# Attention followed by a mixture of experts: routing moved into attention, rows scattered to a table sorted by expert, layer one with stationary weights

## The chip, the cores and the metric

One core of one Trainium2 chip. The metric is device time in microseconds (us) of one execution; the kernel before takes 1046.56 us (median of four runs, 1046.24 to 1047.22). Each kernel was also run once under the hardware profiler; all readings of lines, waits and windows are from that execution. Its span is some 2 us shorter than the time of the run. All runs compared here are in the same state (fast).

## The reference, cut to what matters

```python
# attention: B, H, S, D = 8, 8, 576, 64, causal, with a bias from cumulated s
x = attention(q, k, v, s)                 # brought to (8, 576, 512): 4608 tokens of 512 numbers
logits = x @ w_gate                       # (512, 8): eight experts
local  = sigmoid(x @ w_local)             # (512, 1)
for b in range(8):
    prev_e = -1
    for s in range(576):
        fresh = argmax(logits[b, s])
        e = fresh if s == 0 or local[b, s] < 0.5 else prev_e   # a token may keep its neighbour's expert
        prev_e = e
        p = softmax(logits[b, s])
        out[b, s] = p[e] * (relu(x[b, s] @ w1[e]) @ w2[e])      # w1: 512 x 1024, w2: 1024 x 512, fp32
```

Which expert a token has is known only after its batch is through attention, and where it stands among its expert's tokens only after the batches before it were counted. With these inputs they fill 41 blocks of up to 128 tokens of one expert each (the prediction counts them).

## The kernel before, in its parts that matter

Attention runs over 32 pairs of heads and writes x to a table in device memory, in the order of tokens. Then `route` works on all eight batches at once, mostly on VectorE, and makes four tables for 43 blocks (the largest number that there can be): expert of a block, indices to gather by, indices to scatter by, gates. Then the experts' loop:

```python
def gather(i):                                   # rows of block i, one index for each row, by GpSimd
    xg[i] = gp.tile([P, D], F32, name="xg")
    nc.gpsimd.indirect_dma_start(out=xg[i][:, :], out_offset=None, in_=x_d[:, :],
                                 in_offset=bass.IndirectOffsetOnAxis(ap=idx_g[:, i : i + 1], axis=0))

def layer1(i, half):                             # x stationary, 512 columns of w1 move
    # ... (cut)
    for c in range(DK):
        mm(ps, lhsT=xT[i][:, c, :], rhs=ws[i][0][:, c, f], start=(c == 0), stop=(c == DK - 1))
    nc.scalar.activation(hs[i][:, f], ps, Act.Relu)

def turn_h(i):                                   # eight transposes of h, then copies out of PSUM
    # ... (cut)

def layer2(i):
    # ... (cut) 8 matmuls of 512 columns into ps
    nc.vector.tensor_scalar_mul(y, ps, gate[:, i : i + 1])
    nc.gpsimd.indirect_dma_start(out=out[:, :], ..., in_=y[:, :], ...)   # scatter of y, also by GpSimd

for i in range(NBLK):                            # NBLK = 43
    load(i + 2)                                  # w1 and w2 of the block, 2 MB each, issued by SyncE
    gather(i + 3)
    layer1(i + 1, 0)
    turn_h(i)
    turn_x(i + 2)                                # four transposes of the gathered rows
    layer1(i + 1, 1)
    layer2(i)
```

Note the distance between `gather(i + 3)` and the use of its rows: they are turned by `turn_x(i + 3)`, in the next turn of the loop.

## Time and profile before

| part of the span (1044.4 us) | from, to (us) | what it does |
|---|---|---|
| attention | 0 to 321.7 | TensorE full |
| routing | 321.7 to 378.7 | TensorE mostly idle, half clock |
| experts | 378.7 to 1029.7 | 43 blocks of some 15.05 us, TensorE full |
| tail | 1029.7 to 1044.4 | last y, its scatter, its landing |

The lines for this table are in the prediction. One more reading of the kernel before is wanted for what follows: how long a gather has. Its timeline, TensorE and GpSimd lines picked out (start, length, engine, line, operation, out<-in, count, and in brackets the idle time before with what ended it):

```profile
617.95 0.98 POOL L841 DMA_INDIRECT xg<-x_tokens,idx_g  x1 [0.30 <-issue]
...
619.71 0.60 PE L850 MATMUL xp<-ident,xg 128*128 128x128 f32 x4
...
634.76 0.60 PE L850 MATMUL xp<-ident,xg 128*128 128x128 f32 x4
```

The turn at 619.71 is of an older block; the rows asked for at 617.95 are turned at 634.76. That leaves 16.8 us, and a gather lands in 11.0 as a rule. Its table of waits has one wait of TensorE for gathered rows in the whole run, at the first block (3.4 us).

### The profile page before, as it was taken

The page shows a single profiled execution, that of the slowest core. Times are in us where ns is not written, and L with a number is a line of the kernel's source. Part 1 is how long each engine was busy: PE and PEld are TensorE (multiplying, and loading weights), DVE is VectorE, ACT ScalarE, POOL GpSimd, SP SyncE. Part 2 cuts the span into 40 slices and gives each one's busy share as a digit, 9 for nine tenths or more (in the row PEclk, how much of TensorE's full clock was granted, in tenths as well). Part 3 has the DMA queues.
Part 4 walks back from the last instruction along what each step waited for, and adds up shares of the span by engine and source line. Part 5 has one row for each costly group of instructions (what it writes and reads, how often), then busy time and mean ns, then how long its engine had stood idle before and what let it go on. Part 6 is the DMA issues. An engine that isn't in the chain of part 4 may idle for free.

```text
span 1044.4 us, 12912 instructions
## 1 busy us (share of the span) xinstructions
PE 992.7 (95%) x5028; PEld 593.4 (57%) x5028; DVE 204.7 (20%) x562; ACT 228.0 (22%) x549; POOL 160.4 (15%) x278
## 2 busy tenths in 40 slices
PE   8999999999995659999999999999999999999994
PEld 6778778788884624444444444444444444444441
DVE  3222222222225511111111111111111111111110
ACT  4445454554540001110111111011101110111010
POOL 2212212221220310110111011101111110111000
PEclk9999999999997569999999999999999999999997
DMA  9546336337011089877877887788778778877820
GB/s 283 199 116 220 136 100 225 139 92 228 1 46 46 1 336 427 315 302 304 346 299 289 323 334 286 302 334 314 298 303 347 302 296 312 345 288 301 316 95 3
DMA packets 42934, 249.35 MB, mean 239 GB/s; under 512 B 16845, under 2 KB 16877, under 8 KB 29168
## 3 DMA queue, kind: packets, MB, share of 16 engines
q1 hardware_dynamic: 33952, 226.72, 57.9%
q0 software_dynamic: 7008, 20.74, 5.1%
q10 hardware_dynamic: 1904, 0.98, 0.4%
q8 instruction: 42, 0.69, 0.3%
q14 instruction: 28, 0.23, 0.1%
HBM read 229.54 MB, written 20.71 MB: 240 GB/s over the span
## 4 chain that ended last, share of the span: by engine, by line
PE 92%; DMA 2%; DVE 2%; SPq 2%; POOL 0%; issue 0%; ACT 0%; POOLq 0%; DVEq 0%; ACTq 0%
PE hp L862 29%; PE yp L878 28%; PE po L294 14%; PE ps L243 9%; PE htp L871 4%; PE pot L306 2%; PE xp L850 2%; PE table L795 2%; DMA vTb<-in_vT_dram 2%; SPq L143 1%; DMA w1b<-in_w_dram 1%; PE pot L310 1%; PE vwp L210 1%; PE ps L249 1%; PE vwt L222 0%
## 5 line engine op out<-in xcount | busy, mean ns | idle before, releaser
L862 PE MATMUL hp<-w1b,xT 128*128 128x512 f32 x688 | 312.4, 597 | 5.3 <-DMA w1b<-in_w_dram 4.7
L878 PE MATMUL yp<-w2b,hT 128*128 128x512 f32 x688 | 302.4, 593 | 0.3 <-ACT hT L872 0.3
L878 PEld LDWEIGHTS yp<-w2b,hT 128*128 128x128 f32 x688 | 130.9, 190 | 164.4 <-issue 163.8
L862 PEld LDWEIGHTS hp<-w1b,xT 128*128 128x128 f32 x688 | 128.5, 192 | 151.0 <-issue 149.5
L254 ACT ACTIVATE sc<-ps,bias 128x320 f32<-128x320 f32 (+3 forms) x384 | 151.1, 487 | 158.6 <-PE ps L249 105.2
L863 ACT ACTIVATE hs<-hp 128x512 f32<-128x512 f32 x86 | 51.4, 597 | 613.2 <-PE hp L862 613.2
L294 PEld LDWEIGHTS po<-va,sc 128*128 128x128 f32 x1280 | 147.7, 192 | 20.5 <-issue 20.3
L294 PE MATMUL po<-va,sc 128*128 128x74 f32 x1280 | 156.8, 278 | 0.0
L881 POOL DMA_INDIRECT out_dram<-y,idx_s x43 | 43.6, 1013 | 564.8 <-DVE y L880 564.8
L880 DVE TENSOR_SCALAR y<-yp,gate 128x512 f32<-128x512 f32 x43 | 32.3, 751 | 401.6 <-PE yp L878 401.6
L243 PE MATMUL ps<-qb,kb 64*128 64x320 f32 (+3 forms) x768 | 110.2, 407 | 0.0
L260 POOL TENSOR_SCALAR_AFFINE_SELECT sc<-sc 128x256 f32<-128x256 f32 (+1 forms) x96 | 47.3, 493 | 247.5 <-ACT sc L254 247.5
L243 PEld LDWEIGHTS ps<-qb,kb 64*128 64x128 f32 x768 | 61.9, 189 | 17.5 <-issue 1.9
L872 DVE COPY hT<-htp 128x512 f32<-128x512 f32 x43 | 29.8, 692 | 156.1 <-PE htp L871 156.1
L871 PEld LDWEIGHTS htp<-ident,hs 128*128 128x128 f32 x344 | 40.3, 141 | 22.6 <-issue 22.6
L298 DVE RECIPROCAL recs<-po 128x4 f32<-128x4 f32 x64 | 11.7, 183 | 198.2 <-PE po L294 198.2
L871 PE MATMUL htp<-ident,hs 128*128 128x128 f32 x344 | 44.6, 273 | 0.0
L841 POOL DMA_INDIRECT xg<-x_tokens,idx_g x43 | 42.0, 976 | 13.4 <-issue 13.4
L852 DVE COPY xT<-xp 128x512 f32<-128x512 f32 x43 | 29.3, 681 | 15.2 <-PE xp L850 15.2
L795 PE MATMUL table<-val,place 128*128 128x86 f32 x80 | 17.8, 425 | 12.6 <-POOL val L793 12.6
L850 PE MATMUL xp<-ident,xg 128*128 128x128 f32 x172 | 26.3, 276 | 3.4 <-DMA xg<-x_tokens,idx_g 3.4
L300 DVE TENSOR_TENSOR xb<-po,recs 128x256 f32<-128x256 f32 x64 | 27.2, 425 | 2.2
(131 smaller groups left out, 322.0 us busy)
## 6 DMA issues: line engine op xcount, KB each, us to landing
w1b<-in_w_dram SPq DMA_DIRECT2D x43, 2048.0 KB, 13.4
w2b<-in_w_dram SPq DMA_DIRECT2D x43, 2048.0 KB, 8.3
x_tokens<-xb SPq DMA_DIRECT2D x8, 1024.0 KB, 4.9
qb<-in_q_dram SPq DMA_DIRECT2D x7, 1152.0 KB, 5.2
kb<-in_k_dram SPq DMA_DIRECT2D x7, 1152.0 KB, 7.6
vTb<-in_vT_dram SPq DMA_DIRECT2D x7, 1152.0 KB, 9.8
va<-in_vm_dram SPq DMA_DIRECT2D x7, 1024.0 KB, 7.6
qb<-in_q_dram SPq DMA_DIRECT2D x4, 288.0 KB, 4.7
```

The lines of the kernel that those rows point to most:

```text
L243: mm(ps[:, h, at : at + q1 - q0], lhsT=kb[d, hp, c * P : c * P + P], rhs=qb[d, hp, q0:q1], start=True, stop=True)
L254: nc.scalar.activation(sc[:, h, a:z], ps[:, h, a:z], Act.Exp, bias=bias[:, i : i + 1], scale=scale)
L260: nc.gpsimd.affine_select(out=x, in_=x, compare_op=Alu.is_ge, fill=0.0, base=0, pattern=[[0, 2], [0, len(diag)], [1, P]], channel_multipli ...
L294: mm(po[:, t % 2, h, :], lhsT=weights(n, c, t, h), rhs=va[:, c, 2 * hp + h, :], start=(c == 0), stop=(c == t))
L795: mm(table.rearrange("p k b -> p (k b)"), lhsT=place[:, m - c0, :], rhs=val[:, m].rearrange("p k b -> p (k b)"), start=(m == 0), stop=(m = ...
L841: nc.gpsimd.indirect_dma_start(out=xg[i][:, :], out_offset=None, in_=x_d[:, :], in_offset=bass.IndirectOffsetOnAxis(ap=idx_g[:, i : i + 1] ...
L850: tr(ps[:, c, :], x[:, c * P : (c + 1) * P], ident)
L862: mm(ps, lhsT=xT[i][:, c, :], rhs=ws[i][0][:, c, f], start=(c == 0), stop=(c == DK - 1))
L863: nc.scalar.activation(hs[i][:, f], ps, Act.Relu)
L871: tr(ps[:, j, :], h[:, (g + j) * P : (g + j + 1) * P], ident)
L878: mm(ps, lhsT=h[:, c, :], rhs=ws[i][1][:, c, :], start=(c == 0), stop=(c == FK - 1))
L881: nc.gpsimd.indirect_dma_start(out=out[:, :], out_offset=bass.IndirectOffsetOnAxis(ap=idx_s[:, i : i + 1], axis=0), in_=y[:, :], element_o ...
```

## The change: its intent and its core

The intent is to take the 57 us of routing off the path, two blocks off the 43, and the turns of h off each block:

- Routing is cut into stages and runs for batches 0 to 2 and 3 to 5 inside attention, for batches 6 and 7 inside the first expert steps.
- Rows are scattered, with their index and gate in two more columns, to a table sorted by expert. A block then is 128 contiguous rows, fetched by a plain copy.
- The first block of each of four experts ("early") is complete after six batches, so the experts can start while the last two batches are still being routed. 41 blocks always run, the last two only if needed.
- In layer one the weights are stationary and 128 columns of x move. h comes out already transposed.

```diff
-    attention(tc, q, k, vm, vt, vT, s, w_gate, w_local, x_d, ident, lg, recs)
-    route(tc, ident, lg, ebi, idx_g, idx_s, gate)
-    in_range(tc, recs, out_of)
-    experts(tc, w1, w2, out, x_d, ident, ebi, idx_g, idx_s, gate)
+        for bs, n0, each in (((0, 1, 2), 13, 3), ((3, 4, 5), 25, 3)):
+            g = sort.group(bs, xs)
+            for i, (n, half) in enumerate(((n0, 1), (n0 + 1, 0), (n0 + 1, 1), (n0 + 2, 0), (n0 + 2, 1))):
+                at(n, half, g.stages[i])               # five stages, one in each half step of attention
+            for i, f in enumerate(g.scatters):
+                at(n0 + 3 + i // each // 2, i // each % 2, f)   # then `each` scatters in each half step
+    # ... (cut)
+        experts(tc, w1, w2, out, rows_d, ident, sort,
+                [("early", e) for e in range(EARLY)] + [("further", i) for i in range(SURE)], hooks, wf, first)
+    # ... (cut) the last blocks, under conditions
@@ experts
-    def gather(i):
-        nc.gpsimd.indirect_dma_start(out=xg[i][:, :], out_offset=None, in_=x_d[:, :], ...)
+    def fetch(i):
+        # ... (cut) the block's first row, from a table
+            nc.gpsimd.dma_start(xg[i], rows_d[bass.ds(row, P), :])
@@ layer1
-            mm(ps, lhsT=xT[i][:, c, :], rhs=ws[i][0][:, c, f], start=(c == 0), stop=(c == DK - 1))
-        nc.scalar.activation(hs[i][:, f], ps, Act.Relu)
-    def turn_h(i): ...
+        for j in range(4):
+            f = slice((g + j) * P, (g + j + 1) * P)
+            for c in range(DK):
+                mm(ps[:, j, :], lhsT=w[:, c, f], rhs=xT[i][:, c, :], start=(c == 0), stop=(c == DK - 1))
@@ layer2
         for c in range(FK):
-            mm(ps, lhsT=h[:, c, :], rhs=ws[i][1][:, c, :], start=(c == 0), stop=(c == FK - 1))
+            mm(ps, lhsT=h[:, c, :], rhs=w[:, c, :], start=(c == 0), stop=(c == FK - 1))
+            if c == FK // 2 - 1:
+                turn_x(i + 2)
@@ the loop
-    for i in range(NBLK):
+    for i in range(NBL):
         load(i + 2)
-        gather(i + 3)
         layer1(i + 1, 0)
-        turn_h(i)
-        turn_x(i + 2)
+        fetch(i + 2)
         layer1(i + 1, 1)
         layer2(i)
```

## The prediction

> **What bounds the kernel now.** I read the page first (busy shares, slices), then the table of windows, then the groups, the timeline and the chain for durations, last the DMA landings.
>
> ```profile
> PE 992.7 (95%) x5028; PEld 593.4 (57%) x5028; DVE 204.7 (20%) x562; ACT 228.0 (22%) x549; POOL 160.4 (15%) x278
> PE   8999999999995659999999999999999999999994
> PEclk9999999999997569999999999999999999999997
> ...
> 300.00:320.00 20.00, 20.00 (x193) 17.25 (x189) 4.72 (x21) 8.85 (x24) 5.06 (x16) 1.00 0.01 2
> 320.00:330.00 10.00, 4.57 (x42) 2.72 (x40) 6.20 (x25) 0.49 (x2) 0.00 (x0) 0.81 0.36 118
> 330.00:340.00 10.00, 3.12 (x9) 1.72 (x9) 6.51 (x18) 0.61 (x1) 0.00 (x0) 0.50 0.00 0
> 340.00:350.00 10.00, 1.22 (x6) 1.22 (x6) 7.80 (x16) 0.00 (x0) 3.88 (x4) 0.50 0.00 0
> 350.00:360.00 10.00, 10.00 (x48) 9.88 (x47) 3.75 (x5) 0.00 (x0) 3.13 (x5) 0.50 0.01 2
> 370.00:380.00 10.00, 2.43 (x6) 1.56 (x7) 0.69 (x1) 0.00 (x0) 2.84 (x3) 0.50 0.97 374
> ...
> 600.00:700.00 100.00, 100.00 (x297) 49.13 (x296) 14.28 (x21) 11.69 (x21) 13.92 (x14) 1.00 0.81 314
> ```
>
> Columns of a window: length, then busy time and count of PE, PEld, DVE, ACT, POOL, then clock, DMA share, GB/s. TensorE is the bound in attention (to 321.7 us) and in the experts (from 378.7). Between lies routing, 57 us in which TensorE has little to do and runs at half clock; its busy 350 to 360 is the table matmuls at that clock.
>
> ```profile
> 316.36 4.66 PE L294 MATMUL po<-va,sc 128*128 128x74 f32 x40
> 393.31 0.88 PE htp L871 x8
> 394.19 0.44 PE xp L850 x4
> 394.62 3.44 PE hp L862 x8
> 1014.50 6.87 PE yp L878 x16
> 1029.70 0.75 DVE L880 TENSOR_SCALAR y<-yp,gate 128x512 f32<-128x512 f32 x1 [6.67 <-PE yp L878]
> ```
>
> These are start, length, what, count. One block of 128 tokens costs TensorE 16 layer-one passes (2 x 3.44), 8 turns of h (0.88), 4 turns of x (0.44) and 16 layer-two passes (6.87): 15.07 us. Check: from the first layer-one matmul at 378.7 to the last matmul's end, about 1029.7, are 651 us; 43 x 15.04 = 647, plus some 4 for a cold start. After 1029.7 come 14.7 us of tail (y, its scatter, its landing, the reading of the condition).
>
> **What the Trainium skill says.** (1) "TensorE: Matmul & The Clock Gate", section "LDWEIGHTS (loading the stationary operand)": a load takes columns / 1.2 ns, 107 ns for 128. The trace agrees with it as a spacing: the 40 attention matmuls above, each with new 128-column weights and only 74 moving columns, are (4.66 - 0.28) / 39 = 0.112 us apart (0.278 is the mean of one in the groups), and the turns 0.88 / 8 = 0.110. A record's 190 ns is latency. (2) The same page, Part 1, says that an idle window of about 3.4 us brings the clock to half; the trace has 0.50 from 330 us. (3) "DMA: Bandwidth & Descriptors", "Queues, rings and completion order": an engine takes turns between queues packet by packet. The gathers below agree: 4.2 us when nearly alone, 11.0 as a rule, beside the weights' stream. (4) Its section "SWDGE vs HWDGE vs iDMA" has plain copies from GpSimd go through the same software-made descriptors as indirect ones; nothing in this trace separates the two well.
>
> ```profile
> DMA to landing us min/median/max: 4.2/11.0/12.8
> w1b<-in_w_dram SPq DMA_DIRECT2D x43, 2048.0 KB, 13.4
> w2b<-in_w_dram SPq DMA_DIRECT2D x43, 2048.0 KB, 8.3
> out_dram<-y,idx_s POOLq DMA_INDIRECT x43, 8.5
> wbd<-in_w_gate_dram POOLq DMA_DIRECT2D x2, 8.0 KB, 6.9
> ```
>
> The first line is that of the tile xg, the others give issuer, count, size and median us to landing.
>
> **The change, part by part.**
>
> Blocks. Before, 43 are always run. I counted the tokens of each expert with the reference and its inputs: 573, 516, 565, 575, 717, 459, 513, 690. Rounded up to 128 they make 41 blocks. Each of the four early experts has over 128 tokens in the first six batches, so early blocks add none, and 4 + 37 = 41 is just what runs without a condition; both conditional parts are skipped. Two blocks less: -30 us.
>
> Layer one. Weights stationary gives h already transposed: 64 passes of 128 columns in place of 16 of 512 (two passes for each fp32 matmul). A pass of 512 takes 0.429, so 128 columns stream in 0.107; the load of new weights for each pass, at 0.110 to 0.112, is as long and lies beside the pass before. So 64 x 0.111 = 7.1 against 6.87. The 8 turns of h go: -0.88. A block becomes 7.1 + 0.44 + 6.87 = 14.4 us, 0.64 less; over 41 blocks -26 us. If loads did not hide, it would be near 64 x 0.22 = 14; the 0.112 spacing speaks against it.
>
> Routing. Six batches are routed in attention, where DVE is 28% busy and POOL 19%. TensorE itself gets, per group, 10 + 5 small transposes and 4 matmuls, some 2 us. Each of the ten stages can also hold it for about half a microsecond, by banks taken from the scores' three or by DVE's queue; and batches 4 and 7 reuse a row buffer whose scatters were issued within a step, some 2 us each. I put attention at +10, ending at 332. The store of x goes, and nothing waited for it on TensorE.
>
> Transition. In place of 57 us there is the first fetch. Its buffer lies over attention's, so it is issued after the last attention matmul: 0.3 + issue 0.7 + landing about 5.5 (the first gathers took 4.2 and 8.6) + turns at half clock 1.1 + copy 0.9 = 8.5. First layer-one matmul at 340.5. The gain against 378.7 is 38 us.
>
> Last group and first blocks. Two batches are routed between layer-one steps: 15 transposes, some waits, 5 us. Ten scatters, eight fills and the tables have until the fetch of block 4, over 30 us later, so I expect no wait there.
>
> Weights. Now one tile for w1 and w2, freed only by layer two: load i+2 has one period to bring w1, first in the queue. The first in the queue lands in 8.3 us today, so it does not bind. Bytes per block stay the same: the DMA share would go from 0.81 to 0.85.
>
> Tail. One more condition is read by all engines: 14.7 + 4 = 18.7.
>
> Sum without fetch stalls: 340.5 + 41 x 14.4 + 4 + 5 + 18.7 = 958.6; a run is 2.2 longer than its span: 961.
>
> **The rivals.**
>
> (a) The fetch takes over as the bound of each block. Before, row gathers ran three blocks ahead and were never waited for after the first. Now fetch i+2 stands in GpSimd's order behind the scatter of y of block i-1, and is used in the middle of layer two of block i, 7.1 + 3.4 = 10.5 us after the block began. y takes 1 us, the scatter's issue 1.0, the register's load about 0.6, so it is issued at 2.8 and has 7.7 us. A gather's 11.0 would give a wait of 3.3 us in 37 blocks, +122 us, 1083: slower. Rows of 2056 bytes, not 2048, may make it worse. For a shorter landing speak that the fetch is a plain copy of contiguous rows (a plain GpSimd copy landed in 6.9, small and at the start), and that the turn was moved to the middle of layer two, late enough that it looks fitted to a landing that was watched. I can't settle it from this trace. I choose landing near 8 us and charge 0.3 us to each of 37 blocks, +11.
>
> (b) Weight loads do not hide beside 128-column passes fully: at 0.125 per pass a block is 0.9 longer, +37 us, 1009.
>
> (c) Attention stalls more than I give it: Pool's masks behind scatters, a buffer of rows late. At 2 us in each of 20 half steps, +40, 1010. For it: scatters stand in Pool's queue before the masks. Against: values run one step after scores, so masks have several us of slack.
>
> **Range and chances.** 961 + 11 = 972. The low end is no stall and a cheap transition, 945. The high end has a fetch stall near 2 us, 961 + 74 = 1035. Over 2% faster is under 1025.6: only (a) at nearly full size or two rivals together miss it. Faster 0.86, within 2% 0.08, slower 0.06.
>
> **What would show it.** Right: TensorE at 9 in every slice after one short dip near 335 us; layer-one passes at 0.11 spacing and 14.4 to 14.7 us per block; 64 x 41 layer-one records; no htp. Wrong in (a): turns of x with idle before them released by the DMA of xg, some 37 times, and a block of 16 to 18 us; (b): blocks long without idle time on TensorE; (c): attention ending after 340. A low clock beyond the transition, or the conditional blocks being run, would also break the sum.

## The result, and the profile after

| | median of fast runs, us | range | ratio to before |
|---|---|---|---|
| before | 1046.56 | 1046.24 to 1047.22 | |
| after | 1111.56 | 1109.98 to 1121.75 | 1.064 (1.0586 to 1.0695) |

A ratio here is the mean time of one kernel's fast runs over that of the other's of the same rounds, with a 95% interval, so not quite the ratio of the medians. The change made the kernel 6.4% slower; the prediction was 972 us, with a range to 1035.

The page of the profile after (busy us, share of the span, count; then busy tenths in 40 slices of 28 us; then shares of the chain that ended last; a group with busy us, mean ns | idle before, releaser; two landings with KB each and median us):

```profile
span 1120.1 us, 16042 instructions
...
PE 968.3 (86%) x6538; PEld 710.3 (63%) x6538; DVE 210.6 (19%) x649; ACT 181.8 (16%) x465; POOL 173.9 (16%) x333
...
PE   8999998999989978888888787878888897879785
...
PEclk9999999999998989999999999899999888999898
...
DMA out_dram<-y,at 28%; PE yp L1039 2%; DMA xg<-x_rows 1%; POOLq L1001 1%; PE hp L1027 1%; POOL out_dram L1045 0%; POOL x_rows L937 0%; DVE y L1044 0%; POOLq L1045 0%; PE xp L1010 0%; POOLq L118 0%; POOLq L1003 0%
...
L1010 PE MATMUL xp<-ident,xg 128*128 128x128 f32 x164 | 30.0, 313 | 126.2 <-DMA xg<-x_rows 126.2
...
w<-in_w_dram SPq DMA_DIRECT2D x82, 2048.0 KB, 13.5
xg<-x_rows POOLq DMA_DIRECT2D x41, 257.0 KB, 11.4
```

The hole of routing is gone from the slices (the digits 5, 6 and 5 before, none so low after but the tail's), but from slice 14 on, where the experts are, TensorE has mostly 7 and 8 where it had 9. No engine took its place: DVE, ACT and POOL stand under 20%. The DMA engines did not either; one window in the experts (columns as in the prediction) has their share at 0.66, where before it was 0.81 in a like stretch:

```profile
500.00:600.00 100.00, 83.85 (x485) 60.67 (x484) 11.72 (x21) 3.58 (x6) 9.48 (x12) 0.97 0.66 253
```

The chain on the page leads astray: it puts 28% on the scatters of y, follows them one behind the other, and has only 1% for the fetch. It followed GpSimd's own order back from the end. The table of waits, by tile, says it plainly (us in total, times, longest):

```profile
PE xp L1010 <- DMA xg<-x_rows: 126.2, 38, 6.5
```

TensorE waits 38 times for fetched rows, 126.2 us in all: once for the very first rows (3.8 us, before layer one begins) and 37 times within the blocks (122.4 us). The timeline of a block and a half shows why:

```profile
637.12 3.60 PE L1039 MATMUL yp<-w,hT 128*128 128x512 f32 x8
...
644.97 0.88 PE L1010 MATMUL xp<-ident,xg 128*128 128x128 f32 x4 [4.25 <-DMA xg<-x_rows]
...
645.65 5.08 PE L1039 MATMUL yp<-w,hT 128*128 128x512 f32 x8
...
650.56 7.31 PE L1027 MATMUL hp<-xT,w 128*128 128x128 f32 x64
...
650.76 0.75 DVE L1044 TENSOR_SCALAR y<-yp,xg 128x512 f32<-128x512 f32 x1 [4.12 <-PE yp L1039]
651.79 0.99 POOL L1045 DMA_INDIRECT out_dram<-y,at  x1 [19.00 <-DVE y L1044]
652.78 0.59 POOL L1003 DMA_DIRECT2D xg<-x_rows  x1
```

A block begins at 650.56 with layer one. Only then is the y of the block before ready (650.76), GpSimd issues its scatter (651.79), and the fetch stands behind that scatter in GpSimd's program (652.78). It landed 10.8 us later, at 663.6. TensorE wanted the rows after 7.3 us of layer one and half of layer two, at about 661. This is a closed loop: the end of a block starts the fetch that the middle of the next waits for, so the wait returns in every block and can't be worked off.

The line at 645.65 shows a second cost: after the wait of 4.25 us, eight passes of layer two take 5.08 us; the eight ahead of it, at 637.12, took 3.60. Half clock followed the wait: the trace's record of the granted clock has 0.50 from 645.2 to 648.6.

**Where the time went**, by stages of the two profiled runs:

| stage | before | after | difference |
|---|---|---|---|
| to the first layer-one matmul | 378.7 | 338.9 | -39.8 |
| from there to the last layer-two matmul's end | 651.0 | 768.6 | +117.6 |
| tail | 14.7 | 12.6 | -2.1 |
| span | 1044.4 | 1120.1 | +75.7 |

The 768.6 are 41 blocks of 14.45 us (592.5; the period of a block without a wait, from the first experiment), 122.4 of waits for rows, 2.3 for weights, 3 of cold start, 38.7 of half clock after waits, and some 10 that I did not take apart, the last group's routing among them. The half clock is read from the trace's record of the granted clock: after the cold start TensorE worked 77.4 us of this stage at 0.50, and half of that is lost. Of the 36 blocks that follow the wait for block 4, 19 have such a stretch of half clock and take 19.15 to 21.16 us; the other 17 take 16.66 to 18.45.

### The profile page after: what moved, and what is told of

Read it like the earlier page. It is cut to its first block, busy times and chain, and to the rows that moved or that the text cites. A ratio compares the mean times of both kernels' runs of the same rounds, so it can differ in the third digit from the quotient of the medians.

```text
span 1120.1 us, 16042 instructions
## 1 busy us (share of the span) xinstructions
PE 968.3 (86%) x6538; PEld 710.3 (63%) x6538; DVE 210.6 (19%) x649; ACT 181.8 (16%) x465; POOL 173.9 (16%) x333
## 4 chain that ended last, share of the span: by engine, by line
issue 33%; DMA 29%; PE 2%; POOLq 1%; POOL 0%; DVE 0%
DMA out_dram<-y,at 28%; PE yp L1039 2%; DMA xg<-x_rows 1%; POOLq L1001 1%; PE hp L1027 1%; POOL out_dram L1045 0%; POOL x_rows L937 0%; DVE y L1044 0%; POOLq L1045 0%; PE xp L1010 0%; POOLq L118 0%; POOLq L1003 0%
## 5 line engine op out<-in xcount | busy, mean ns | idle before, releaser
L1039 PE MATMUL yp<-w,hT 128*128 128x512 f32 x656 | 329.5, 651 | 0.0
L1027 PEld LDWEIGHTS hp<-xT,w 128*128 128x128 f32 x2624 | 302.1, 193 | 22.7 <-issue 21.3
L1027 PE MATMUL hp<-xT,w 128*128 128x128 f32 x2624 | 303.6, 277 | 3.2 <-DMA w<-in_w_dram 2.3
L1039 PEld LDWEIGHTS yp<-w,hT 128*128 128x128 f32 x656 | 131.9, 211 | 141.6 <-issue 141.6
L1045 POOL DMA_INDIRECT out_dram<-y,at x41 | 40.8, 996 | 673.0 <-DVE y L1044 620.5
L1010 PE MATMUL xp<-ident,xg 128*128 128x128 f32 x164 | 30.0, 313 | 126.2 <-DMA xg<-x_rows 126.2
L307 PE MATMUL ps<-qk 64*128 64x320 f32 (+3 forms) x768 | 110.3, 406 | 0.3 <-ACT sct L329 0.3
L1030 DVE TENSOR_SCALAR hT<-hp 128x512 f32<-128x512 f32 x41 | 28.4, 692 | 251.7 <-PE hp L1027 251.7
L307 PEld LDWEIGHTS ps<-qk 64*128 64x128 f32 x768 | 61.1, 187 | 18.1 <-issue 1.7
L1044 DVE TENSOR_SCALAR y<-yp,xg 128x512 f32<-128x512 f32 x41 | 30.8, 751 | 149.5 <-PE yp L1039 149.5
L937 POOL DMA_INDIRECT x_rows<-xb,r_slot_i x32 | 31.5, 984 | 9.1 <-issue 8.0
## 6 DMA issues: line engine op xcount, KB each, us to landing
xg<-x_rows POOLq DMA_DIRECT2D x41, 257.0 KB, 11.4
```

The lines of the kernel that those rows point to most:

```text
L307: mm(ps[:, h, at : at + q1 - q0], lhsT=kb[d, hp, c * P : c * P + P], rhs=qb[d, hp, q0:q1], start=True, stop=True)
L937: self.s.nc.gpsimd.indirect_dma_start(out=next(self.s.views)[:, :], out_offset=bass.IndirectOffsetOnAxis(ap=self.slot[:z, m : m + 1], axis=0),
L1010: tr(ps[:, c, :], xg[i][:, c * P : (c + 1) * P], ident)
L1027: mm(ps[:, j, :], lhsT=w[:, c, f], rhs=xT[i][:, c, :], start=(c == 0), stop=(c == DK - 1))
L1030: nc.vector.tensor_scalar_max(hT[i][:, g : g + 4], ps, 0.0)
L1039: mm(ps, lhsT=h[:, c, :], rhs=w[:, c, :], start=(c == 0), stop=(c == FK - 1))
```

## The experiments

My theory: the fetch is issued too late for how long it takes beside the weights' stream, and all else in the change is worth what the sum said. The rival: stationary weights, or the routing within attention, cost more than was thought. The first four went to one chip together, the other three to another together (the kernel before: 1047.28 and 1046.64 us there).

### e2_order: the scatter of y issued behind the next fetch

GpSimd's program was: scatter y0, scatter y1, fetch 4, scatter y2, fetch 5, and so on. With the scatter of y moved one turn back, it is: scatter y0, fetch 4, scatter y1, fetch 5. Each fetch is issued one block earlier, and nothing else changes.

```diff
 def layer2(i):
-        y = gp.tile([P, D], F32, name="y")
+        y = ys[i] = gp.tile([P, D], F32, name="y")
         nc.vector.tensor_scalar_mul(y, ps, xg[i][:, D + 1 : D + 2])
-        nc.gpsimd.indirect_dma_start(out=out[:, :], ..., in_=y[:, :], ...)
+    ys = {}
+    def put(i):
+        y = ys.pop(i)
+        nc.gpsimd.indirect_dma_start(out=out[:, :], ..., in_=y[:, :], ...)
 for i in range(NBL):
     load(i + 2)
     layer1(i + 1, 0)
     fetch(i + 2)
+    if i:
+        put(i - 1)
     layer1(i + 1, 1)
     layer2(i)
+put(NBL - 1)
```

> The changed kernel with one order turned round: the scatter of y of block i-1 is issued by GpSimd after the fetch of block i+2, not before it. No buffer, no byte and no TensorE instruction is added. Theory (the fetch is issued too late for its landing of 11.4 us): the fetch no longer waits for y, it goes out nearly a block earlier, the waits of the turns of x for the DMA of xg (130 us in 39 times) go but for block 4, whose rows must first be scattered, and with them the half clock that follows them; a block falls from 18.5 to 14.5 us and the run from 1111 to 955 to 975 us. Rival (the sixteen DMA engines can't carry weights, rows and y of a block in 14.5 us, the late fetch only shows it): blocks stay above 17 us, waits move to the weights w, the time stays above 1080.

Measured: 962.15 us (955.94 to 966.62), ratio 0.9176 (0.913 to 0.9223), right result. Its waits, its window and its timeline:

```profile
PE xp L1010 <- DMA xg<-x_rows: 3.7, 1, 3.7
```

```profile
500.00:600.00 100.00, 100.00 (x580) 72.88 (x579) 15.36 (x28) 4.18 (x7) 11.06 (x14) 1.00 0.84 324
```

```profile
652.95 7.31 PE L1027 MATMUL hp<-xT,w 128*128 128x128 f32 x64
...
655.17 0.59 POOL L1003 DMA_DIRECT2D xg<-x_rows  x1
...
663.53 0.60 PE L1010 MATMUL xp<-ident,xg 128*128 128x128 f32 x4
...
663.97 3.60 PE L1039 MATMUL yp<-w,hT 128*128 128x512 f32 x8
```

The 38 waits have become one, that for the first rows (a wait for block 4, which I had expected, did not come); in this window TensorE is full at full clock, and the DMA share is 0.84, as before the change. The rows asked for at 655.17 are now for the turn one block later, at 678: 22.8 us instead of some 8. Thirty-six blocks in a row take 14.45 us each. Turning the order of two instructions on GpSimd took the loss away.

### e3_turn_late: the other end of the same distance

The issue stays late, and the rows are turned after seven of layer two's eight chunks instead of four, 2.6 us later.

```diff
-            if c == FK // 2 - 1:
+            if c == FK - 2:
                 turn_x(i + 2)
```

> The changed kernel with the turn of x of block i+2 moved from after 4 of the 8 chunks of layer two to after 7 of them: needed 2.6 us later, nothing else moved, no DMA touched. Theory (the wait is landing minus need: 3.1 us now): waits fall to 0.5 us or less, too short to bring the clock down, the copy of xT then costs some 0.3 us of its own before layer one; blocks of 15.0 to 15.5 us, the run at 980 to 1010 us. Rival (DMA throughput): no change, above 1090. Rival (the landing itself follows the period): waits stay near 3 us.

Measured: 989.5 us (986.66 to 997.95), ratio 0.9457 (0.9403 to 0.9511), right result.

```profile
PE xp L1010 <- DMA xg<-x_rows: 18.6, 23, 3.8
```

Of 126.2 us of waits 18.6 are left: 3.8 for the first rows, the others between 0.2 and 1.5 us, so about half of them above the 0.5 that was expected. So giving 2.6 us more at the end of the distance takes nearly all of it away, without touching the order on GpSimd. The waits were a shortage of some 3 us in each block, no more.

### e4_half_weights: the landing without the full weights' stream

Only w1 of each block is loaded; layer two uses the first block's w2. The result is wrong (relative error 1.32).

```diff
-    for a, src in ((0, w1), (DK * F, w2)):
+    for a, src in ((0, w1), (DK * F, w2))[: 1 if half else 2]:
@@ load
-        ws[i] = (wf if wf and i % 3 == 0 else wp).tile(...)
-        load_weights(nc, ws[i], w1, w2, j)
+        ws[i] = wp.tile(...)
+        load_weights(nc, ws[i], w1, w2, j, half=wf is not None)
@@ layer2
-        w = ws[i][:, DK * F :]
+        w = (first if wf else ws[i])[:, DK * F :]
```

> Wrong result on purpose: in the first 41 blocks only w1 is loaded for each block, layer two uses the w2 of the first expert throughout. The order of issues is that of the changed kernel. Theory (the fetch lands late because its packets take turns with the packets of the weights' stream, sent at the same moment): with half the stream the fetch lands some 3 to 5 us earlier, near 7 us from issue, the waits fall under 0.5 us and the run to 955 to 985 us. Rival (a GpSimd copy behind the scatter of y needs 11 us of its own): landing stays at 11, run near 1110.

Measured: 967.67 us (963.58 and 971.76), ratio 0.9237 (0.919 to 0.9284). Waits and window:

```profile
PE xp L1010 <- DMA xg<-x_rows: 8.4, 2, 4.6
```

```profile
500.00:600.00 100.00, 100.00 (x584) 73.26 (x583) 14.98 (x28) 4.18 (x7) 11.09 (x14) 1.00 0.51 178
```

With the weights' traffic halved the fetch, issued as late as in the changed kernel, is in time; the two waits left are for the first rows (3.8 us) and for block 4 (4.6 us). From the trace's records of single packets, a fetch is 64 packets of 4112 bytes (two rows of 2056). In the changed kernel, in e2_order and in e3_turn_late alike, its first packet comes 6.5 us after the issue and its last at about 10.4 (medians); here the first comes at 1.6 and the last at 2.8, earlier than the 7 us that I had expected.

The same records show what the fetch stands behind. The 64 packets of the scatter of y, issued 1 us before it, run first in the same queue: in the changed kernel from 3.5 to 6.6 us after the fetch's issue, here from 0.6 to 1.2. In the kernel before, a gather stood behind a scatter in the same way (128 packets, from 3.2 to 10.0 us). While the fetch's own packets run, about 1.3 packets of weights, 16 KB each, go for one of them. That fits turns taken packet by packet; what the first 3.5 us are spent on stays open. e2_order left this as it is: its fetch still stands behind a scatter, only one block earlier.

What this doesn't settle: since layer two no longer holds the tile, it is free half a block sooner, and the load's place in time moves too. Here a fetch runs with no weights in flight at all. So the weights' stream makes the landing long; what the scatter's packets ahead of the fetch cost by themselves, no run has tested.

### e5_before_layer1: stationary weights alone, on the kernel before

```diff
-            mm(ps, lhsT=xT[i][:, c, :], rhs=ws[i][0][:, c, f], start=(c == 0), stop=(c == DK - 1))
-        nc.scalar.activation(hs[i][:, f], ps, Act.Relu)
+        for j in range(4):
+            f = slice((g + j) * P, (g + j + 1) * P)
+            for c in range(DK):
+                mm(ps[:, j, :], lhsT=ws[i][0][:, c, f], rhs=xT[i][:, c, :], start=(c == 0), stop=(c == DK - 1))
+        # relu into hT, one half on ScalarE and one on VectorE
-            turn_h(i)
```

> The kernel before with layer one alone changed: weights stationary, 64 passes of 128 columns in place of 16 of 512, and the turns of h gone; 43 blocks, gathers and routing as before. Theory (each pass 0.112 us, loads hidden): a block from 15.05 to 14.45 us, 43 x 0.6 = 26 us less, 1046.6 to about 1021. Rival (loads of weights don't hide or the denser stream lowers the clock): same or slower.

Measured: 1021.0 us (1019.96 to 1024.04), ratio 0.9742 (0.9726 to 0.9759), right result: 26 us less, as the prediction's own term for this part has it.

```profile
500.00:600.00 100.00, 100.00 (x580) 73.22 (x579) 14.25 (x20) 3.75 (x7) 13.93 (x14) 1.00 0.83 324
```

580 matmul records in 100 us where the kernel before has about 297, and TensorE full at full clock: loads of new weights for each pass do hide. This is against the prediction's rival (b), and against stationary weights as the cause of the loss.

### e6_before_41: two blocks less, on the kernel before

```diff
-NBLK = N // P + E - 1
+NBLK = N // P + E - 1 - 2
```

> The kernel before with 41 blocks in place of 43, nothing else (valid for these inputs, whose tokens fill exactly 41 blocks). Theory: two blocks of 15.05 us less, 1046.6 to 1016.5; the tables of the routing get 4 columns narrower, under 1 us. Rival (empty blocks are cheap, or the last blocks hide something): less than 20 us gained.

Measured: 1015.71 us (1014.69 to 1016.46), ratio 0.9703 (0.9688 to 0.9718), right result (these inputs need 41 blocks; in general this is no correct kernel). 31 us less.

With the first experiment the parts add up: -31 for two blocks, -25 for layer one (0.60 for each of 41 blocks), and the first layer-one matmul of e2_order at 344.4 instead of 378.7, -34. That is -90 against -85 measured. The difference lies mostly in the first blocks of e2_order, one of which takes 21.12 us: from 376 to 381 us single matmuls of layer one stand over 1 us apart there, released by nothing that the profile shows, and half clock follows.

### e7_spread: e2_order, and the scatters spread over more half steps

In e2_order attention ends later than before, by 16.7 us, about 10 of it in the half steps in which three scatters each are issued. (The profiles of the five runs with this same attention have 11.2 to 19.1.) The changed kernel's timeline shows one such place:

```profile
188.42 0.98 POOL L937 DMA_INDIRECT x_rows<-xb,r_slot_i  x1 [0.28 <-issue]
...
189.71 0.97 POOL L937 DMA_INDIRECT x_rows<-xb,r_slot_i  x1 [0.30 <-issue]
190.98 0.97 POOL L937 DMA_INDIRECT x_rows<-xb,r_slot_i  x1 [0.30 <-issue]
191.97 0.43 POOL L324 TENSOR_SCALAR_AFFINE_SELECT sc<-sc 128x256 f32<-128x256 f32 x1
192.46 1.77 PE L359 MATMUL po<-va,sc 128*128 128x74 f32 x7 [3.71 <-POOL sc L324]
```

Three scatters stand one behind the other on GpSimd at 1.3 us each, the mask of the scores comes after them, and TensorE waits 3.71 us for that mask. So the scatters were spread, one or two in a half step, with one more buffer for the rows that live longer.

```diff
-        keep = main.enter_context(tc.tile_pool(name="keep", bufs=4))
+        keep = main.enter_context(tc.tile_pool(name="keep", bufs=5))
-        for bs, n0, each in (((0, 1, 2), 13, 3), ((3, 4, 5), 25, 3)):
+        for bs, n0, each in (((0, 1, 2), 13, 1), ((3, 4, 5), 25, 2)):
```

> The turned order (scatter of y behind the next fetch) and, in attention, the scatters of rows one (first group) or two (second group) in a half step in place of three, for which the rows get a fifth buffer. Theory (in the runs so far attention ends 11 to 19 us later than in the kernel before; 2 us of it per group are routing's own work on TensorE, the rest comes while scatters stand in GpSimd's queue, whose masks wait for their landings): pairs 16 to 18 and 28 to 30 lose under 2 us in place of 4 to 10, attention ends 4 to 8 us later than before, the run at 948 to 958. Rival (those losses are DVE's routing work or banks of PSUM): attention as late as in e2_order, run at 956 to 967. A risk: the second group's last scatters land later and the first fetch waits for them, some 3 us.

Measured: **949.79 us** (948.51 to 953.47, five runs), ratio 0.9076 (0.9063 to 0.909), right result. It beats both kernels. Attention now ends 4.9 us later than before, and the half steps with scatters cost TensorE nothing that I could find. Two things were changed at once, though, the spread and the fifth row buffer, and which of them took the loss away is not shown. The losses before lay in pairs 16, 17, 28 and 29, where batches 4 and 7 take over a row buffer, and in the largest one of e2_order (7.9 us, near 300 us) the profile shows no wait for a mask, but VectorE waiting 4.4 us for something that it doesn't name. Slices of its page (24 us each):

```profile
PE   8999999999999899899999999999999999999994
...
PEclk9999999999999989899999999999999999999997
```

Two digits of 8 are left after the start: one at the end of attention, where the first rows are fetched, and one near 390 us, where the fetch of the first late block is waited for once (4.2 us) and brings half clock for some us. Open is a further wait: this kernel's table of waits still has GpSimd seven times, 19.7 us in all, at a mask of the tail's scores for scatters to land. They cost TensorE little there, and I did not take them apart.

### e8_warm: the changed kernel, with filler before each waiting turn

If the waits bring the clock down, TensorE kept busy meanwhile should not lose that. Eight matmuls of the identity into a spare bank stand before each turn that waits. They take some 1.9 us of a wait of 3.

```diff
+            if wf and c == FK // 2 - 1 and 4 <= i + 2 < NBL:
+                warm = bank(1)[0]
+                for _ in range(8):
+                    mm(warm[:, :P], lhsT=ident, rhs=ident, start=True, stop=True)
             if c == FK // 2 - 1:
                 turn_x(i + 2)
```

> The changed kernel, with its late fetch, plus 8 matmuls of the identity (16 passes of 128 columns, some 1.8 us, result unused) before each turn of x that waits. They fit into the wait (3.1 us), so a block should not get longer by them, and TensorE's idle time falls to some 1.3 us. Theory (the blocks of 19 to 21 us are those in which the wait brought the clock to half, those of 17.5 are the wait alone): all blocks become 17.4 to 17.9 us, the granted clock in the expert stage 1.00, the run at 1065 to 1085, 30 to 45 us less than 1111, with more work. Rival (the long blocks come from DMA or the loads of weights): blocks stay between 17 and 21 and the run near 1111 or above.

Measured: 1091.2 us (1084.33 to 1095.61), ratio 1.0403 (1.0375 to 1.0432), right result. That is 20 us less than the changed kernel by doing more, but 6 us above what I had expected.

```profile
PE xp L1010 <- DMA xg<-x_rows: 59.5, 37, 5.0
```

After block 4 the mean block is 18.12 us (the median 17.86): 14.45, the filler 1.95, a wait of 1.41 and 0.3 of half clock. Six of 36 blocks still have half clock, and take over 20 us. The mean clock of the profiled run is 0.976, against 0.951. The waits fell by 66.7 us, about what the filler takes, so the idle time was only filled. The half clock after waits costs 12.8 us in place of 38.7, and those 26 us are the difference of the two profiled runs. So the waits' effect on the clock is real and was part of the loss; the filler prevents most of it, not all.

## Why the prediction was wrong, point by point

**What held.** The sum without fetch stalls was 961 us; e2_order, which is the change with those stalls taken away, ran in 962.15. That the two are within 2 us is partly luck: in its profile the first layer-one matmul came 3.9 us later than in the sum and the blocks, with their start, took 4.8 more, while the tail took 6 less. Term by term:

| term | predicted | measured |
|---|---|---|
| two blocks less | -30 | -31 (e6_before_41) |
| layer one | -26 (0.64 in 41 blocks) | -26 (e5_before_layer1: 0.60 in 43 blocks) |
| spacing of layer-one passes | 0.111 | 0.1116 (7.31 us for 64) |
| a block without a wait | 14.4 | 14.45 |
| first layer-one matmul | 340.5 | 338.9 after, 344.4 in e2_order |
| attention's delay | +10 | +11.2 after, +16.7 in e2_order |
| tail | 18.7 | 12.6 |

The tail's extra condition cost nothing that shows, and the time had been charged for it. Rival (b) is refuted. Rival (c) is there in kind, at about the size that the sum already had for attention. (Rivals (b) and (c) are added to 972 and (a) to 961; 972 + 40 is 1012, not 1010.) The conditional blocks were not run: there are 2624 layer-one records, 64 x 41.

**The step that failed** is in rival (a): "I choose landing near 8 us and charge 0.3 us to each of 37 blocks, +11." The rival's working was right in all but this choice. Its fetch was issued 2.2 us after the block began (2.8 had been worked out), and was wanted about 10.7 after. The landing was 11.4 as a median, as long as the gather's 11.0 that stood in the profile before, and not 8. In e2_order the same fetch, with 22.8 us to land in, costs nothing.

Two arguments had moved the choice from 11 to 8. One was a plain copy that landed in 6.9 us: 8 KB, issued at the start, beside other loads (DMA share 0.79 in the first 10 us) but not beside the weights' stream, and with no scatter ahead of it. The gathers of the same profile, of nearly the same size, beside the same stream and like the fetch behind a scatter of y, were the better measure. The fetch's packets fit that: 6.5 of its 11.4 us pass before the first of them, 3.1 of these on the packets of the scatter. The rival had counted this scatter by its 1.0 us of issue alone. Without it the fetch would land near 8.3 us (11.4 less 3.1; an estimate, no run did this). The other was that the turn's place "looks fitted to a landing that was watched". That is a guess about whoever wrote the change, and no reading of a trace. It should have had no weight; without it, I think, the odds between 8 and 11 would have gone the other way, and the expected time over 1046.

**A size that was off** even in the rival's own account: it gives 1083, and 1111.56 came, 28 more (in the slower profiled run 39 more). The waits in the blocks are 122.4 us, the 122 that it had. What it lacks is the half clock that follows such waits, 38.7 us in the profiled run. The prediction cites the skill's window of about 3.4 us, and uses it for the transition alone; a wait of 3.3 us in each block was next to that figure and was not held against it. The length of a wait does not decide alone: one of 3.81 us kept full clock, one of 2.80 lost it. In this trace all stretches of half clock begin on one grid of 3.41 us. Laid on that grid, the 20 intervals of the expert stage after which the clock fell have TensorE idle for 2.05 us or more, and all others at full clock for 1.98 or less; in e8_warm the figures are 2.06 (7 intervals) and 2.02. So a wait costs the clock when enough of it falls into one interval. This limit is that of the blocks: before block 4 of e4_half_weights 1.63 us sufficed. e8_warm shows the part of the clock by itself.

## What to carry to other kernels

When a transfer is moved closer to its use, work out its distance from the instruction that the issuing engine must do first, and set against it the landing of a like transfer under the same load in the profile, not that of a small one elsewhere in the run. Here the DMA queue kept its order too, so count the packets of what was issued just before. A scatter that waits for a result, put ahead of a fetch in one engine's program, ties the fetch to that result and closes a loop over the blocks; issuing the fetch first cost nothing here and turned +6.4% into -8.2%. And a wait of about 3 us in each block cost more than its own length here, 1.05 us more on average, because the clock dropped behind half of them.

## What the Trainium skill lacked or had wrong

- "DMA: Bandwidth & Descriptors", section "Anatomy of one DMA — SWDGE (gpsimd) path": its fit, 2.0 us + bytes / 436e3, gives an estimate of 2.6 us for the fetch's 257 KB. With no weights in flight (e4_half_weights) the last packet came 2.8 us after the issue, which is near it; beside the weights' stream the fetch landed in 11.4. The section has no landing under load: 3.5 us to the queue's first packet, 3.1 for the packets of the scatter ahead, about 3.9 for its own and 0.9 from the last packet to the landing.
- "TensorE: Matmul & The Clock Gate", Part 1, puts half clock after at least one idle window of about 3.4 us and calls the window free-running. The traces have a grid of 3.41 us, but a window need not be idle throughout: in the blocks here 2.05 us of idle time in one sufficed, and 1.98 did not. The half clock cost 38.7 us over 37 waits, 1.05 us each.
- The same page, section "Back-to-back issue gap": its sustained spacing of about 81 ns for N = 128, which names no data type, is not what fp32 layer-one passes showed: 0.1116 us each. That is nearer to its 107 ns for loading 128 columns, but a quarter of a pass of 512 columns is 0.107 us too (0.429 / 4), so the runs do not tell which of the two sets the spacing.
